# Gathering the ordered token ids with 48 and 16 rows in place of 43 and 2

## The chip, the cores and the metric

The program runs on one core of one Trainium2 chip. The time is the device time of one execution in microseconds (us). One execution is recorded by the hardware profiler; it has a span, from the first to the last instruction, and a time of its own that includes what lies around the span.

## What is computed

An attention layer with landmarks feeds a layer of experts in which each token goes to the one expert with the largest logit:

```python
# attention: q, k, v are (8, 8, 576, 64); 32 landmarks are means over 18 rows
A = softmax(q @ k_lm.T / 8); Bm = softmax(q_lm @ k_lm.T / 8); C = softmax(q_lm @ k.T / 8)
Z = Bm.T / (norm1(Bm) * norminf(Bm) + 1e-6)
for _ in range(6):
    Z = 2 * Z - Z @ Bm @ Z
x = (A @ Z @ C @ v)                        # then as rows: (4608, 512)
# experts: w_gate (512, 8), w1 (8, 512, 1024), w2 (8, 1024, 512)
expert_idx = argmax(x @ w_gate, axis=1)
gate_w = softmax(x @ w_gate)[arange(4608), expert_idx]
for e in range(8):
    mask = expert_idx == e
    out[mask] = gate_w[mask, None] * (relu(x[mask] @ w1[e]) @ w2[e])
```

## The kernel before

**First stage, up to about 259 us.** The attention is computed in 18 periods, pipelined over the 8 batches. Each batch writes its rows of x to a scratch tensor in HBM (`xs`) by plain transfers that SP issues. The order of the instructions in this stage is made by a scheduler that places them by its own estimate of times. In the last part of it (the tail of the attention) the orders of PE and SP are written out by hand.

**The table of ordered ids.** As soon as the logits of a batch are there, `tokens` works out for each token its place in a table `order` in HBM: 8 experts by 4608 places, 16 floats a place (the token's id, its gate weight, and zeros). `scatter` (L594) writes 96 places at a time from POOL, 6 such transfers a batch. 128 places in a row are one *block* of 8 KB, so a block holds the ids and gates of one tile of 128 tokens, all of one expert. The table has 288 blocks.

**Reading it back.** `rows_in` (L638 to L643) gathers whole blocks into SBUF by an indirect transfer from POOL: the list `at` has a block number for each partition, and block `at[p]` lands in partition `p` of the tile `room`. It is called twice. The early call, after 4 of the 8 batches, fetches the blocks of 2 tiles (`EARLY`) into `ids_early`. The other call, after the last scatter, fetches one block for each of up to 43 tiles (`SLOTS` = 36 + 8 - 1) into memory that later holds the second buffer of `ht`; in the trace it is `ht<-order,s_at`, in the early one `ids_early<-order,early_at`.

`rows` then turns the ids into row numbers for the gathers of x: four operations on DVE (L652, tile `r`), four transposes on PE (L656), a copy to integers on DVE (L659, tile `read`); later two more transposes (L666, L667) and copies (L670, L672) give the rows to write to and the gates.

**Second stage.** `Experts` goes over the tiles (slots). A slot's 128 rows of x are gathered by four indirect transfers from POOL (L820, into `xg` or `xe`), transposed in blocks on DVE (L833, `buf`), split into a high and a low part by ACT (L835) and DVE (L838, `xt`), and multiplied on PE with `w1` (`up`, L852, `ps_tp` and `ps_fi`). The relu on ACT (L870) and DVE (L872) gives `h`, which is turned in the same way to `ht`, multiplied with `w2` (`down`, `ps_fr` and `ps_ch`), scaled by ACT (L882) and scattered to the output by POOL (L883). Slots 0 and 1 use what the early call found; all others need the second gather. The weights of an expert are fetched by SP (L782, `raw`) and split by ACT (L796) and DVE (L797).

Between the two stages the order of all five engines is written by hand. On PE: `up` of slots 0 and 1, then the transposes of the ids, then `down` of slot 0. On DVE the operations L652 of the second gather stand ahead of L838 of slot 0, without which `down` of slot 0 can't begin. On POOL the gather stands behind the last scatter, and ahead of all gathers of x for slots 2 and up.

Of the kernel before, what the change touches and what calls it, by code (L numbers as in the profile page):

```python
# [12 lines left out]
F32 = mybir.dt.float32  # L13
# [19 lines left out]
REC = 16  # L33
# [22 lines left out]
def done(g):  # L56
    for _ in g:
        pass
# [422 lines left out]
EARLY = 2  # L481
# [4 lines left out]
class Routing:  # L486
# [150 lines left out]

    def rows_in(self, at, n):  # L638

        room = self.room[n][:n]  # L640
        self.ids = room.rearrange("p (a o) -> p a o", o=REC)
        self.nc.gpsimd.indirect_dma_start(out=room, out_offset=None, in_=self.blocks,
                                          in_offset=bass.IndirectOffsetOnAxis(ap=at[:n], axis=0))  # L643

    def rows(self, n, pad):

# [304 lines left out]
def moe(tc, q, k, v, wg, w1, w2, out):  # L951
    nc = tc.nc
    with ExitStack() as ctx, ExitStack() as late:
# [5 lines left out]
        with ExitStack() as zero:  # L959
            routing = Routing(tc, ctx, zero, psum, order)  # L960
        experts = Experts(tc, ctx, psum, routing, xs, w1, w2, out)
        experts.weights(ctx, 0)
        with ExitStack() as front:
            attention = Attention(tc, ctx, front, psum, q, k, v, wg)
            attention.tokens, attention.groups = routing.tokens, routing.groups
            attention.xs = [xs[S * b:S * b + S].rearrange("(p j) c -> p j c", j=J) for b in range(B)]
            routing.ident = attention.ident
            routing.room = {EARLY: front.enter_context(tc.tile_pool(name="r_ids", bufs=1)).tile([EARLY, REC * 128], F32, name="ids_early")}
            for i in range(2 * B + 2):
                extra = []  # L970
                if routing.scatters:
                    extra.append((routing.scattered(), J, 0))
                if i == ROWS:
                    done(routing.rows(EARLY, None))
                    extra.append((experts.start(), 8, 0))
                if i == 17:
                    extra.append((experts.split(0, 512, nc.vector), 8, 0))
                attention.period(i, B, extra)
                if i in CLEAR:
                    with tc.issue_after(attention.loads["v"].ins):  # L980
                        for e in CLEAR[i]:
                            routing.clear(e)
                if i == FETCH:
                    experts.fetch(0, routing.first[0:1, 0:1])
# [5 lines left out]
        with tc.manual_schedule(engines=engines):  # L990
# [12 lines left out]
            room = experts.buf[2].rearrange("p a c -> p (a c)")  # L1003
# [74 lines left out]
```

## Time and profile before

| | |
|---|---|
| median of 3 runs | 701.17 us (700.9 to 701.24) |
| the profiled execution, its own time | 700.81 us |
| its span | 699.0 us |
| PE busy | 647.4 us (93% of the span) |
| DVE busy | 521.5 us (75%) |
| ACT busy | 398.9 us (57%) |
| POOL busy | 345.2 us (49%) |
| HBM traffic | 124 GB/s over the span |

PE is the TensorE matmul engine, PEld its weight loads, DVE VectorE, ACT ScalarE, POOL GpSimd, SP SyncE. The profiled execution is 0.36 us below the median, and its span is 1.81 us shorter than its time; both differences are taken to stay as they are.

### The profile page before, as it was taken

What the parts mean: (1) busy time and instruction counts of PE and PEld (TensorE: products, weight loads), DVE (VectorE), ACT (ScalarE), POOL (GpSimd) and SP (SyncE); (2) the same over time, 40 slices, a digit from 0 to 9 for tenths busy, and PEclk for the clock granted to TensorE, in tenths of its full rate; (3) what the DMA queues carried; (4) which work ended last, traced back from release to release, by engine and by line L of the source; (5) the groups of instructions that cost most, each with busy time, mean ns of one, the idle gap of its engine ahead of it and who ended that gap; (6) DMA issues with size and microseconds to landing.
All of it is one profiled execution on the core that took longest, in us unless ns stands there. A gap on an engine that the chain in (4) does not pass through costs nothing.

```text
span 699.0 us, 13809 instructions
## 1 busy us (share of the span) xinstructions
PE 647.4 (93%) x4511; PEld 510.9 (73%) x4511; DVE 521.5 (75%) x1359; ACT 398.9 (57%) x983; POOL 345.2 (49%) x372
## 2 busy tenths in 40 slices
PE   7899989998898881999999999999999999999996
PEld 4676777666675661777888888888888888888884
DVE  4788876988878671667789879857599789866653
ACT  4776766575645461245577566645467477544442
POOL 4554546575363460777655354443536445351231
PEclk9999997998979995899999999999999999999999
DMA  9997766776342530146233423511143343310110
GB/s 221 292 276 178 205 159 146 197 200 207 96 111 59 181 85 20 60 144 224 72 121 122 137 92 128 166 51 43 57 155 116 105 137 107 126 62 31 31 49 30
DMA packets 47002, 87.35 MB, mean 125 GB/s; under 512 B 8642, under 2 KB 27074, under 8 KB 46851
## 3 DMA queue, kind: packets, MB, share of 16 engines
q1 hardware_dynamic: 36336, 65.30, 32.7%
q0 software_dynamic: 10560, 20.87, 9.5%
q8 instruction: 38, 0.62, 0.4%
q14 instruction: 68, 0.56, 0.3%
HBM read 64.61 MB, written 22.05 MB: 124 GB/s over the span
## 4 chain that ended last, share of the span: by engine, by line
PE 46%; DMA 3%; issue 3%; POOL 1%; DVE 1%; ACT 0%; POOLq 0%; DVEq 0%
PE ps_fi L852 12%; PE ps_ch L852 12%; PE ps_tp L852 11%; PE ps_fr L852 11%; DMA xe<-xs,read 3%; DVE h L872 0%; POOL xg L820 0%; POOL out_dram L883 0%; POOL xe L820 0%; DVE buf L833 0%; DVE ht L838 0%; ACT ht L835 0%; POOLq L918 0%; POOLq L883 0%; DVEq L833 0%
## 5 line engine op out<-in xcount | busy, mean ns | idle before, releaser
L883 POOL DMA_INDIRECT out_dram<-buf,write x38 | 39.0, 1026 | 166.0 <-ACTq L809 140.4
L820 POOL DMA_INDIRECT xg<-xs,read x80 | 83.7, 1046 | 42.3 <-issue 22.4
L820 POOL DMA_INDIRECT xe<-xs,read x84 | 88.0, 1047 | 25.7 <-issue 23.8
L835 ACT CAST ht<-buf 128x512 fp32r<-128x512 f32 x76 | 47.1, 622 | 87.9 <-DVE buf L833 86.9
L852 PE MATMUL ps_fr<-whi,ht 128*128 128x512 f32 x304 | 96.6, 399 | 0.0
L852 PE MATMUL ps_ch<-whi,ht 128*128 128x512 f32 x304 | 94.4, 392 | 2.4 <-ACTq L809 2.4
L852 PE MATMUL ps_tp<-whi,xt 128*128 128x512 f32 x304 | 83.2, 395 | 1.5 <-ACTq L809 1.5
L872 DVE TENSOR_SCALAR h<-ps_tp 32x256 f32<-32x256 f32 x152 | 64.2, 422 | 27.1 <-PE ps_tp L852 24.6
L872 DVE TENSOR_SCALAR h<-ps_fi 32x256 f32<-32x256 f32 x144 | 60.8, 422 | 28.8 <-PE ps_fi L852 26.5
L852 PE MATMUL ps_fi<-whi,xt 128*128 128x512 f32 x288 | 78.1, 393 | 0.0
L870 ACT ACTIVATE h<-ps_tp 32x256 f32<-32x256 f32 x152 | 57.1, 376 | 36.2 <-PE ps_tp L852 32.5
L870 ACT ACTIVATE h<-ps_fi 32x256 f32<-32x256 f32 x144 | 54.1, 376 | 34.8 <-PE ps_fi L852 31.0
L852 PEld LDWEIGHTS ps_ch<-whi,ht 128*128 128x128 f32 x304 | 57.0, 188 | 15.3 <-ACTq L809 3.2
L852 PEld LDWEIGHTS ps_fr<-whi,ht 128*128 128x128 f32 x304 | 58.2, 192 | 13.1 <-DVE ht L838 0.5
L852 PEld LDWEIGHTS ps_tp<-whi,xt 128*128 128x128 f32 x304 | 56.9, 188 | 14.2 <-ACTq L809 1.9
L852 PEld LDWEIGHTS ps_fi<-whi,xt 128*128 128x128 f32 x288 | 54.1, 188 | 11.8
L852 PE MATMUL ps_fr<-wlo,ht 128*128 128x512 f32 x152 | 60.5, 398 | 0.0
L852 PE MATMUL ps_ch<-wlo,ht 128*128 128x512 f32 x152 | 59.5, 391 | 0.0
L594 POOL DMA_INDIRECT order<-i_tok,l_at x48 | 45.5, 948 | 26.1 <-issue 11.2
L797 DVE TENSOR_TENSOR wlo<-raw,whi 128x512 fp32r<-128x512 f32 (+1 forms) x64 | 49.9, 834 | 5.7 <-ACT whi L796 5.7
L838 DVE TENSOR_TENSOR ht<-buf,ht 128x512 fp32r<-128x512 f32 x76 | 51.1, 692 | 3.8 <-ACT ht L835 0.2
L833 DVE STREAM_TRANSPOSE buf<-h 128x512 f32<-128x512 f32 x76 | 49.7, 690 | 5.6 <-DMA out_dram<-buf,write 1.8
(274 smaller groups left out, 1326.3 us busy)
## 6 DMA issues: line engine op xcount, KB each, us to landing
raw<-in_moe_w_dram SPq DMA_DIRECT2D x48, 512.0 KB, 5.8
ld_k<-in_k_dram SPq DMA_DIRECT2D x14, 576.0 KB, 5.3
ld_q<-in_q_dram SPq DMA_DIRECT2D x14, 576.0 KB, 7.7
ld_v<-in_v_dram SPq DMA_DIRECT2D x14, 576.0 KB, 5.0
xs<-xrow SPq DMA_DIRECT2D x40, 192.0 KB, 2.3
order<-zero SPq DMA_DIRECT2D x8, 288.0 KB, 10.7
xe<-xs,read POOLq DMA_INDIRECT x84, 2.6
xg<-xs,read POOLq DMA_INDIRECT x80, 2.8
```

Source lines behind the costliest of these rows:

```text
L594: self.nc.gpsimd.indirect_dma_start(out=self.places[n + j], out_offset=bass.IndirectOffsetOnAxis(ap=at[:, j:j + 1], axis=0), in_=self.tok[ ...
L797: (engine or nc.vector).tensor_tensor(out=l, in0=x, in1=h.bitcast(F32), op=ALU.subtract)
L820: self.nc.gpsimd.indirect_dma_start(out=x[:, t, :], out_offset=None, in_=src.rearrange("n (q c) -> (n q) c", q=4), in_offset=bass.Indirect ...
L833: nc.vector.transpose(out=x.rearrange("p c (t j) -> p t c j", t=4), in_=src[:, :, 32 * c:32 * c + 128].rearrange("p t (c i) -> p t c i", c=4))
L835: nc.scalar.copy(out=hi[:, c:c + 4, :], in_=x)
L838: nc.vector.tensor_tensor(out=lo[:, c:c + 4, :], in0=x, in1=hi[:, c:c + 4, :].bitcast(F32), op=ALU.subtract)
L852: nc.tensor.matmul(ps[c // 512] if type(ps) is list else ps[:, c // 512], lhsT=x0[:, a, :], rhs=w[:, a, c:c + 512], start=a == 0 and j == ...
L870: nc.scalar.activation(out=dst, in_=src, func=AF.Relu)
L872: nc.vector.tensor_scalar(out=dst, in0=src, scalar1=0.0, scalar2=None, op0=ALU.max)
L883: nc.gpsimd.indirect_dma_start(out=self.outs[s], out_offset=bass.IndirectOffsetOnAxis(ap=at, axis=0), in_=y, in_offset=None, bounds_check= ...
```

## The change

The length of the gathered list is rounded up to a multiple of 16: the second gather fetches 48 blocks into 48 partitions in place of 43, the early one 16 in place of 2, and the early tile has 16 partitions in place of 2. The added blocks are read and never used; everything that reads the tiles still takes 43 and 2 rows (`room[:n]`). The list `at` has 128 entries in both cases. An added entry is a valid block number: behind the last tile it is the number of its partition.

```diff
     def rows_in(self, at, n):
 
-        room = self.room[n][:n]
-        self.ids = room.rearrange("p (a o) -> p a o", o=REC)
+        m = -(-n // 16) * 16
+        room = self.room[n][:m]
+        self.ids = room[:n].rearrange("p (a o) -> p a o", o=REC)
         self.nc.gpsimd.indirect_dma_start(out=room, out_offset=None, in_=self.blocks,
-                                          in_offset=bass.IndirectOffsetOnAxis(ap=at[:n], axis=0))
+                                          in_offset=bass.IndirectOffsetOnAxis(ap=at[:m], axis=0))
...
-            routing.room = {EARLY: front.enter_context(tc.tile_pool(name="r_ids", bufs=1)).tile([EARLY, REC * 128], F32, name="ids_early")}
+            routing.room = {EARLY: front.enter_context(tc.tile_pool(name="r_ids", bufs=1)).tile([16, REC * 128], F32, name="ids_early")}
```

On POOL and SP no instruction changes its place. Here is POOL between the two stages, before (`order` is the table, `l_at` the places, `ht` the tile gathered into, `xg` and `xe` the rows of x):

```order
L594 DMA order<-i_tok,l_at 36864x16 x18
L642 DMA ht_4098<-order,s_at 43x2048
L820 DMA xg_4088<-xs,read_4417 128x128 x4
L820 DMA xg_4089<-xs,read_4417 128x128 x4
L883 DMA out_dram<-buf_4091,write_4461 4608x512
```

And with the change; the file is one line longer, so that L642 is L643 and L820 is L821:

```order
L594 DMA order<-i_tok,l_at 36864x16 x18
L643 DMA ht_4098<-order,s_at 48x2048
L821 DMA xg_4088<-xs,read_4417 128x128 x4
L821 DMA xg_4089<-xs,read_4417 128x128 x4
L884 DMA out_dram<-buf_4091,write_4461 4608x512
```

Only the size of the gather differs. In the first stage, from the early gather on, the scheduler orders PE, DVE and ACT a little differently. The first such place that matters for the last gather is DVE at the tail of the attention, where the places `l_at` of batch 5 are made, for which POOL's last run of scatters waits. Before (`l_t`, `l_mx` lead to `l_at`, `buf` holds rows of x or logits, `xt` the split rows of slots 0 and 1, `st` a tile of the values stage):

```order
L580 TENSOR_TENSOR l_t<-ps_fi,i_base 96x48
L339 TENSOR_TENSOR rp<-rp,ps_tp 128x2x32
L415 STREAM_TRANSPOSE buf_4093<-ps_fi 96x192
L838 TENSOR_TENSOR xt_4094<-buf_4091,xt_4094 128x512
L587 TENSOR_TENSOR acc<-acc,l_n 96x8
L279 COPY st<-ps_fr 128x8
L581 TENSOR_TENSOR l_t<-l_t,l_oh 96x48
L554 TENSOR_REDUCE l_mx<-buf_4093 96x6
L838 TENSOR_TENSOR xt_4095<-buf_4092,xt_4095 128x512
L582 TENSOR_REDUCE l_mx<-l_t 96x6
L555 TENSOR_TENSOR buf_4093<-buf_4093,l_mx 96x6x8
L583 CAST l_at<-l_mx 96x6
```

With the change:

```order
L580 TENSOR_TENSOR l_t<-ps_fi,i_base 96x48
L834 STREAM_TRANSPOSE buf_4091<-xe_144 128x4x4x32
L581 TENSOR_TENSOR l_t<-l_t,l_oh 96x48
L834 STREAM_TRANSPOSE buf_4092<-xe_145 128x4x4x32
L339 TENSOR_TENSOR rp<-rp,ps_tp 128x2x32
L582 TENSOR_REDUCE l_mx<-l_t 96x6
L415 STREAM_TRANSPOSE buf_4093<-ps_fi 96x192
L839 TENSOR_TENSOR xt_4094<-buf_4091,xt_4094 128x512
L583 CAST l_at<-l_mx 96x6
L554 TENSOR_REDUCE l_mx<-buf_4093 96x6
L839 TENSOR_TENSOR xt_4095<-buf_4092,xt_4095 128x512
```

L554, the second split of x (L838, now L839), L555 and an L279 stood ahead of `l_at` and now stand behind it; the two L833 (now L834) stood ahead of it in both. A little later on DVE the places `l_at` of batch 6 and the tile `w` of batch 7 are made, before (`wlo` is the split of `w2`):

```order
L580 TENSOR_TENSOR l_t<-ps_fi,i_base 96x48
L797 TENSOR_TENSOR wlo_4084<-raw_4082,whi_4083 128x512
L581 TENSOR_TENSOR l_t<-l_t,l_oh 96x48
L582 TENSOR_REDUCE l_mx<-l_t 96x6
L797 TENSOR_TENSOR wlo_4084<-raw_4082,whi_4083 128x512
L583 CAST l_at<-l_mx 96x6
L797 TENSOR_TENSOR wlo_4084<-raw_4082,whi_4083 128x512
L364 TENSOR_TENSOR w<-ps_ch,m_187 128x256 x2
```

With the change:

```order
L580 TENSOR_TENSOR l_t<-ps_fi,i_base 96x48
L581 TENSOR_TENSOR l_t<-l_t,l_oh 96x48
L582 TENSOR_REDUCE l_mx<-l_t 96x6
L798 TENSOR_TENSOR wlo_4084<-raw_4082,whi_4083 128x512
L583 CAST l_at<-l_mx 96x6
L364 TENSOR_TENSOR w<-ps_ch,m_187 128x256 x2
L798 TENSOR_TENSOR wlo_4084<-raw_4082,whi_4083 128x512 x2
```

One split of weights stands ahead of `l_at` in place of two, and one ahead of `w` in place of three. In the second stage the order of DVE differs in one pair (the second L838 of an early slot stands behind the first L872, not ahead of it).

## Rows read from the trace of the kernel before

**Rows 1.** The chain that ended last: start us, duration us, engine tile line.

```profile
317.54 5.73 PE ps_ch L852 x24
...
631.42 5.52 PE ps_fi L852 x24
```

**Rows 2.** Who waited for whom over the execution: us in total, times, longest us.

```profile
PE ps_fi L656 <- DVE r L652: 17.4, 1, 17.4
DVE r L652 <- DMA ht<-order,s_at: 15.5, 1, 15.5
POOL xg L820 <- DVE read L659: 18.4, 1, 18.4
```

**Rows 3.** Timeline, 259 to 279 us: start us, us, instruction, [idle before it <- releaser].

```profile
259.15 1.45 POOL L642 DMA_INDIRECT ht<-order,s_at  x1 [2.30 <-DVE h L872]
259.25 1.30 DVE L833 STREAM_TRANSPOSE buf<-h 128x512 f32<-128x512 f32 x2
261.23 3.17 ACT L870 ACTIVATE h<-ps_sc 32x256 f32<-32x256 f32 x8
276.08 1.18 DVE L652 SCALAR_TENSOR_TENSOR r<-ht,i_quarter 43x128 f32<-43x128 f32 x4 [15.53 <-DMA ht<-order,s_at]
...
279.01 0.97 POOL L820 DMA_INDIRECT xg<-xs,read  x1 [18.40 <-DVE read L659]
```

**Rows 4.** Windows between the stages: length, busy by engine, PEclk, DMA share, GB/s.

```profile
262.00:263.20 1.20, 0.00 (x0) 0.00 (x0) 0.00 (x0) 1.13 (x3) 0.00 (x0) 0.99 0.02 7
263.20:275.50 12.30, 0.00 (x0) 0.00 (x0) 0.00 (x0) 1.13 (x3) 0.00 (x0) 0.50 0.06 27
276.50:283.60 7.10, 7.02 (x19) 5.09 (x20) 6.07 (x17) 0.00 (x0) 3.68 (x4) 0.50 0.10 30
```

**Rows 5.** DMA queues and issues, 260 to 277 us: packets, MB, share of 16 engines.

```profile
q0 software_dynamic: 704, 0.35, 7.1%
ht<-order,s_at POOLq DMA_INDIRECT x1, 16.9
```

**Rows 6.** The same, 171.4 to 180.4 us, the early gather.

```profile
q0 software_dynamic: 32, 0.02, 1.3%
```

**Rows 7.** The same, 278.9 to 283.9 us, four gathers of x.

```profile
q0 software_dynamic: 96, 0.20, 13.0%
xg<-xs,read POOLq DMA_INDIRECT x4, 2.5
```

**Rows 8.** Timeline of DVE where the early ids are used.

```profile
180.41 0.34 DVE L652 SCALAR_TENSOR_TENSOR r<-ids_early,i_quarter 2x128 f32<-2x128 f32 x1
180.68 0.14 DVE L393 TENSOR_TENSOR l<-l,ps_fi 96x8 f32<-96x8 f32 x1
```

**Rows 9.** Timeline of POOL, 233 to 308 us.

```profile
233.92 0.94 POOL L594 DMA_INDIRECT order<-i_tok,l_at  x1 [8.95 <-DVE l_t L560]
241.42 1.11 POOL L594 DMA_INDIRECT order<-i_tok,l_at  x1 [0.45 <-DVE l_at L583]
255.94 0.92 POOL L594 DMA_INDIRECT order<-i_tok,l_at  x1 [0.30 <-issue]
...
306.36 0.94 POOL L820 DMA_INDIRECT xe<-xs,read  x1 [0.30 <-issue]
```

**Rows 10.** Timeline of DVE and PE, 308 to 318 us.

```profile
308.91 0.71 DVE L833 STREAM_TRANSPOSE buf<-xe 128x512 f32<-128x512 f32 x1 [4.30 <-DMA xe<-xs,read]
...
310.43 1.19 PE L852 MATMUL ps_tp<-whi,xt 128*128 128x512 f32 x4 [1.48 <-ACTq L809]
```

**Rows 11.** Timeline of DVE in the tail of the attention.

```profile
232.64 0.68 DVE L838 TENSOR_TENSOR xt<-buf,xt 128x512 fp32r<-128x512 f32 x1
233.47 0.17 DVE L583 CAST l_at<-l_mx 96x6 int32<-96x6 f32 x1
239.13 0.69 DVE L797 TENSOR_TENSOR wlo<-raw,whi 128x512 fp32r<-128x512 f32 x1 [3.04 <-ACT whi L796]
240.99 0.16 DVE L583 CAST l_at<-l_mx 96x6 int32<-96x6 f32 x1
```

## The prediction

> **What bounds the kernel now.** I read the chain that ended last first, to see which stretch is closed. From 317.54 us on it is PE alone, one product of 24 matmuls behind the other up to 637 us [rows 1]; nothing there can be gained by a faster transfer, but all of it starts earlier if the stretch ahead of it does. So I looked for the longest waits of PE in the list of waits. One stands out: 17.4 us for `r` on DVE, and DVE in its turn waits 15.5 us for the second gather of ids, POOL 18.4 us for what is made of it [rows 2]. It is one wait, seen by three engines.
>
> The timeline shows it from the inside [rows 3]. POOL issues the gather at 259.15, DVE is done with what it can do without it at 260.55 (259.25 + 1.30), ACT at 264.4 (261.23 + 3.17), and `r` starts at 276.08, 16.93 us after the issue. From there everything follows in a fixed order: POOL's first gather of x comes 2.93 us later, at 279.01.
>
> Why is the gather so slow? Between 263.2 and 275.5 the DMA engines are busy to a share of 0.06, which is 1 of 16, and move 27 GB/s [rows 4]. The queue's packets tell the same: 704 [rows 5]. 43 blocks on one engine, a small filler packet for each of them on the 15 others (645), and one completion packet on each of 16 make exactly 704. The early gather of 2 blocks has 32 packets [rows 6]: 2 blocks on 2 engines, 14 fillers, 16 completions; on one engine it would be 2 + 30 + 16 = 48. A gather of 128 rows of x has 32 (96 in a stretch with three of them) [rows 7], 16 of data and 16 completions. So 43 rows, a prime number, ran on 1 engine, 2 on 2 and 128 on 16.
>
> The Trainium skill, "DMA: Bandwidth & Descriptors", section "Why a DMA increments its semaphore by 16 and not by 1", says that the number of engines is the largest number up to 16 that divides the slowest dimensions of both sides; the trace agrees, with 1 engine for 43 rows. It also names an exception for some direct copies, which would have put 43 rows on 15 engines; the 704 packets speak against that here.
>
> **The change part by part.** *The second gather.* 48 rows spread over 16 engines are 3 blocks on each in place of 43 on one. A block takes 8,192 bytes / 27 GB/s = 0.303 us on one engine [rows 4]. No row shows this transfer, so I bound it from both sides.
> - Slow end: the same transfer without 40 of its 43 blocks on the busiest engine, 16.93 - 40 x 0.303 = 4.8 us from issue to landing.
> - Fast end: a gather of x lands 2.5 us after its issue [rows 7], with 4 KB an engine (0.15 us at 27 GB/s); with 24 KB (0.91 us) it is 2.5 + 0.76 = 3.3 us.
>
> The first is nearer, being the same transfer, but its issue took 1.45 us on POOL [rows 3], against 0.97 for a gather of x, which I put down to its 704 packets; 64 packets should save about half a microsecond of it. I take 4.2 us. DVE then starts `r` at 259.15 + 4.2 = 263.35, behind its own 260.55, so the wait shrinks to 2.8 us and doesn't vanish. Gain: 16.93 - 4.2 = **12.7 us**, between 12.1 and 13.6. The five added blocks are in this; on DVE and PE nothing gets larger.
>
> The skill's same page, section "Anatomy of one DMA", fits 2.0 us plus bytes / 436e3. For 393,216 bytes that would be 2.9 us, an estimate from that page, and the sum would be 1.3 us better than mine; for the 352,256 bytes of before it gives 2.8 us against the 16.93 measured, so it holds at best for a transfer that is spread.
>
> *What is behind it.* DVE's and PE's steps from `r` on are the same, and ACT is free at 264.4, before DVE's next `h` is due. POOL's gathers of x start 2.93 us after `r` as before, and then POOL issues transfer upon transfer, 22 from 279.01 to 306.36 (1.3 us each), the last of them the rows of slot 5 [rows 3, 9]. DVE waits 4.30 us for these rows at 308.91, and PE, whose next operand stands behind that on DVE, idles 1.48 us at 310.43 [rows 10]. So POOL, not PE, carries the shift through, and it carries all of it. What is late next is POOL's row of gathers.
>
> *The clock of PE.* After the last matmul PE's granted clock stayed at 1.00 (2.4 GHz) to 263.2 us and was at 0.50 (1.2 GHz) from there through 283.6, 7 us after PE resumed [rows 4]. PE would now resume at about 263.9, near the moment at which it fell. If the clock stays up, PE does its 7.1 us of half-clock work up to 3.5 us faster, but then it waits that much longer at the place of rows 10. I cost it at nothing; the cover is POOL's row of issues.
>
> *The early gather.* 16 blocks of 8 KB on 16 engines in place of 2 on 2. Its landing is not waited for: DVE takes `r` at 180.41 behind other work, 9 us after the issue [rows 8]. The 14 added blocks (115 KB) run at a time when the queues are full; at 16 engines x 27 GB/s they hold the others up by at most 0.3 us. Taken at nothing; the cover is those 9 us.
>
> *The scheduler's other order.* That is the part of the change that isn't meant. In the tail the last gather can't be issued before the last scatter (255.94) has landed, and the 18 scatters run back to back on POOL from 233.92, when the first `l_at` (233.47) is there [rows 9, 11]. In the new order four DVE operations that stood ahead of this first `l_at` stand behind it (an L838 of 0.68 us [rows 11], and an L279, an L554 and an L555 of 0.15 to 0.20), so it comes up to 1.2 us earlier. The next group's `l_at` (240.99) stood behind two splits of weights, the first of which waited 3.04 us for ACT [rows 11]; now it stands behind one, and so is ready about 1.1 us earlier too. Against that, PE's last matmuls on `v`, after which SP may fetch `w2` into that memory, stand a few instructions later in PE's new order. I take **0.7 us** gained. But from the early gather on (171 us) DVE, PE and ACT run in another order for 60 us, with clock and waits following from it, and no row prices that: I allow 3 us either way.
>
> *Sum.* 700.81 - 12.7 - 0.7 = 687.4 us for the profiled execution (span 685.6). The median of before is 0.36 above its profile, so the forecast is **687.8 us**.
>
> **The rivals.**
> 1. *The gather still runs on one engine* (slower than before). If the number of engines came from something else than the count of rows, such as the size of a block, 48 blocks would take 5 x 0.303 = 1.5 us more: 701.17 + 1.5 - 0.7 = 702.0, or 702.7 if the other order gives nothing. It decides at one question, whether 48 rows are divided by 16; the counts for 2, 43 and 128 rows speak against it. Chance 0.04.
> 2. *The first stage gives part of it back.* If the new order costs more than 3 us ahead of the last scatter, because a `l_at` or the fetch of `w2` comes late, the time is 688.5 + 3 to 688.5 + 7: 691.5 to 695. For it speaks that PE, DVE and ACT wait for one another there at every step; against it that the two places I could follow both move forward. Chance 0.10.
> 3. *PE carries the end after all and its clock stays up.* Then up to 3.5 us of the half-clock stretch come on top: 687.8 - 3.5 = 684.3. Against it stands the idle time of PE in rows 10, which shows that POOL is later. Chance 0.05.
>
> **How the numbers follow.** The forecast has a chance of 0.81; by its own terms (12.1 to 13.6 gained on the gather, the order 0.7 gained give or take 3) it goes from 684 to 692, most of it within 686 to 690. The likeliest single time is 687.8. The range that holds 8 in 10 reaches into rival 2 and rival 3: **684.7 to 691.8**. A difference under 0.2% (1.4 us) can't be told from no change in this kernel. Faster by more than that: the forecast, rivals 2 and 3, 0.95; within 0.2%: 0.02, half of rival 1's prices; slower: 0.03.
>
> **What would show it.** Right: the second gather has 64 packets, the DMA share over its time is several tenths, and it lands 3.3 to 4.8 us after its issue; DVE's wait for it falls from 15.5 to about 2.8 us and PE's for `r` from 17.4 to about 4.7; the first gather of x comes 2.9 us after `r`; PE still idles over 1 us ahead of `up` of slot 4. The issue of the second gather moves by the first stage's part, forecast 0.7 us earlier. Wrong: a DMA share of 0.06 again (rival 1), an issue of the gather at 262 us or later (rival 2), or PE without that idle time and its clock at 1.00 throughout (rival 3).

## The result, and the profile after

The changed kernel takes 690.75 us (median of four runs, 688.39 to 692.17) against 701.03 of the kernel before beside it (four runs, 698.57 to 701.24); the ratio is 0.9853, with a 95% interval of 0.9823 to 0.9883. The forecast was 687.8 us, with a range of 684.7 to 691.8. The profiled execution took 688.39 us and has a span of 686.6 us, 12.4 us less than before. All lines from L640 on carry a number that is one higher.

The list of waits, with the three rows that answer to [rows 2]:

```profile
POOL xg L821 <- DVE read L660: 7.4, 1, 7.4
PE ps_fi L657 <- DVE r L653: 5.7, 1, 5.7
DVE r L653 <- DMA ht<-order,s_at: 3.8, 1, 3.8
```

All three are 11 to 12 us shorter, and none is gone. The timeline that answers to [rows 3]:

```profile
258.90 0.90 POOL L643 DMA_INDIRECT ht<-order,s_at  x1 [2.17 <-issue]
259.13 1.30 DVE L834 STREAM_TRANSPOSE buf<-h 128x512 f32<-128x512 f32 x2
261.11 3.18 ACT L871 ACTIVATE h<-ps_sc 32x256 f32<-32x256 f32 x8
264.26 1.19 DVE L653 SCALAR_TENSOR_TENSOR r<-ht,i_quarter 43x128 f32<-43x128 f32 x4 [3.83 <-DMA ht<-order,s_at]
...
267.18 0.96 POOL L821 DMA_INDIRECT xg<-xs,read  x1 [7.38 <-DVE read L660]
```

The gather now is on POOL for 0.90 us in place of 1.45, and `r` starts at 264.26, **5.36 us after the issue** in place of 16.93. This time, from POOL's issue of the gather to the start of `r`, is called the landing below. POOL's first gather of x follows 2.92 us after `r`, as before (2.93). The DMA view of the 5.5 us from the issue to just behind `r` (the two upper rows are 40 slices of 0.14 us: busy share of the 16 engines in tenths, and GB/s), which answers to [rows 4, 5] (a packet counts in the slice in which it begins):

```profile
DMA  0000000002099985559947940030000000000000
GB/s 0 0 0 0 0 0 0 0 0 60 0 298 417 179 238 179 119 119 536 238 60 119 238 60 0 0 60 0 0 0 0 0 0 0 0 0 0 0 0 0
...
q0 software_dynamic: 64, 0.39, 34.9%
```

There are 64 packets, 48 of data and 16 completions, as forecast. 34.9% of 16 engines over 5.5 us are 30.7 us of packets: **0.64 us for a block** at most, where one engine alone took 0.303. POOL's scatters ahead of the gather and the last gather of x behind it, which answer to [rows 9]:

```profile
233.93 1.25 POOL L594 DMA_INDIRECT order<-i_tok,l_at  x1 [10.88 <-DVE l_mx L554]
...
255.81 0.92 POOL L594 DMA_INDIRECT order<-i_tok,l_at  x1 [0.30 <-issue]
...
294.39 0.94 POOL L821 DMA_INDIRECT xe<-xs,read  x1 [0.30 <-issue]
```

The waits of DVE and PE ahead of the chain, and the chain, which answer to [rows 1, 10]:

```profile
296.94 0.71 DVE L834 STREAM_TRANSPOSE buf<-xe 128x512 f32<-128x512 f32 x1 [4.26 <-DMA xe<-xs,read]
...
298.46 1.21 PE L853 MATMUL ps_tp<-whi,xt 128*128 128x512 f32 x4 [1.50 <-ACTq L810]
...
305.42 0.72 PE L853 MATMUL ps_ch<-whi,ht 128*128 128x512 f32 x2 [1.18 <-ACTq L810]
```

```profile
305.42 5.75 PE ps_ch L853 x24
...
619.17 5.53 PE ps_fi L853 x24
```

Everything here is shifted as a whole: POOL's last gather for slot 5 by 11.97 us (306.36 to 294.39), DVE's wait for the rows of slot 5 by 11.97 us (308.91 to 296.94), PE's wait behind it by 11.97 (310.43 to 298.46), the start of the chain that is PE alone by 12.12 (317.54 to 305.42), the end by 12.4. PE's wait ahead of slot 4 is the same, 1.50 us against 1.48.

In one place PE's clock is lower than before. The windows of the changed kernel (busy time of PE, PEld, DVE, ACT and POOL with their counts; then PE's granted clock, the share of the DMA engines, GB/s):

```profile
226.30:233.10 6.80, 6.80 (x81) 4.89 (x79) 4.64 (x16) 2.72 (x7) 0.00 (x0) 0.55 0.13 23
261.00:264.50 3.50, 0.00 (x0) 0.00 (x0) 0.24 (x1) 3.09 (x9) 0.00 (x0) 0.53 0.35 68
264.50:271.00 6.50, 6.24 (x16) 4.57 (x16) 6.13 (x16) 0.00 (x0) 2.91 (x4) 0.50 0.07 23
271.00:284.00 13.00, 13.00 (x59) 10.49 (x59) 8.27 (x24) 3.79 (x6) 10.13 (x10) 0.98 0.21 66
```

From 226.3 to 233.1, in the tail of the attention, the clock was at 0.55 on average, so mostly at 1.2 GHz. The same window of the kernel before has it at 1.00:

```profile
226.30:233.10 6.80, 6.68 (x103) 5.46 (x103) 6.80 (x28) 3.72 (x11) 0.00 (x0) 1.00 0.33 97
```

What stands ahead of it on PE is a wait that the kernel before hasn't got:

```profile
225.42 0.78 PE L321 MATMUL ps_tp<-rp 128*128 128x160 f32 x4 [1.15 <-DVE l_m L562]
```

After the gather the clock fell as before, but only to about 271, not to 283.6.

### The profile page after: what moved, and what is told of

Read it like the earlier page. It is cut to its first block, busy times and chain, and to the rows that moved or that the text cites. A ratio compares the mean times of both kernels' runs of the same rounds, so it can differ in the third digit from the quotient of the medians.

```text
span 686.6 us, 13812 instructions
## 1 busy us (share of the span) xinstructions
PE 647.9 (94%) x4511; PEld 509.9 (74%) x4511; DVE 520.8 (76%) x1359; ACT 398.9 (58%) x983; POOL 343.9 (50%) x372
## 3 DMA queue, kind: packets, MB, share of 16 engines
q1 hardware_dynamic: 36336, 65.30, 33.1%
## 4 chain that ended last, share of the span: by engine, by line
PE 46%; DMA 4%; issue 3%; DVE 1%; POOL 1%; ACT 0%; POOLq 0%; DVEq 0%
PE ps_fi L853 12%; PE ps_ch L853 12%; PE ps_tp L853 11%; PE ps_fr L853 11%; DMA xg<-xs,read 4%; DVE h L873 0%; POOL out_dram L884 0%; POOL xg L821 0%; DVE buf L834 0%; DVE ht L839 0%; ACT ht L836 0%; POOLq L919 0%; POOLq L884 0%; DVEq L834 0%; DVEq L810 0%
## 5 line engine op out<-in xcount | busy, mean ns | idle before, releaser
L821 POOL DMA_INDIRECT xe<-xs,read x84 | 87.5, 1042 | 25.7 <-issue 24.1
L821 POOL DMA_INDIRECT xg<-xs,read x80 | 83.7, 1046 | 31.3 <-issue 21.8
L594 POOL DMA_INDIRECT order<-i_tok,l_at x48 | 45.7, 952 | 27.7 <-issue 11.5
L839 DVE TENSOR_TENSOR ht<-buf,ht 128x512 fp32r<-128x512 f32 x76 | 51.0, 691 | 3.8 <-ACT ht L836 0.2
L834 DVE STREAM_TRANSPOSE buf<-h 128x512 f32<-128x512 f32 x76 | 49.7, 692 | 4.9 <-DMA out_dram<-buf,write 1.0
```

The source lines that it names most:

```text
L594: self.nc.gpsimd.indirect_dma_start(out=self.places[n + j], out_offset=bass.IndirectOffsetOnAxis(ap=at[:, j:j + 1], axis=0), in_=self.tok[ ...
L821: self.nc.gpsimd.indirect_dma_start(out=x[:, t, :], out_offset=None, in_=src.rearrange("n (q c) -> (n q) c", q=4), in_offset=bass.Indirect ...
L834: nc.vector.transpose(out=x.rearrange("p c (t j) -> p t c j", t=4), in_=src[:, :, 32 * c:32 * c + 128].rearrange("p t (c i) -> p t c i", c=4))
L839: nc.vector.tensor_tensor(out=lo[:, c:c + 4, :], in0=x, in1=hi[:, c:c + 4, :].bitcast(F32), op=ALU.subtract)
```

## The experiments

Two theories. **Mine:** the number of engines that carry the second gather is the largest number up to 16 that divides its rows; going from 1 to 16 is the whole gain, and what is behind it only shifts. **Rivals:** part of the gain (rival A), or a loss that hides some of it (rival B), is in the early gather and in the other order of the first stage; or the size of the list counts and not its divisors (rival C); or PE's clock, not POOL's transfers, carries the end (rival 3 of the prediction).

Where a group of kernels ran side by side, the kernel before ran among them. Its mean was 698.64 us (17 runs) for the first group and 699.49 (11 runs) for the third. The second group fell on a chip on which the kernel before took 752 us and the gather was issued at 290 to 294 us; I use only landings and ratios from it.

**1. The two parts apart.** One kernel with 48 rows in the second gather and 2 in the early one, whose order in the first stage is that of the kernel before; one with 16 in the early gather and 43 in the second, whose order is that of the changed kernel; and the changed kernel again.

The edit for the second gather of 48 alone (the early tile has its 2 partitions again):

```diff
-        m = -(-n // 16) * 16
+        m = 2 if n == EARLY else 48
```

> Only the second gather takes 48 rows, the early one stays at 2, and the order of the first stage is that of the kernel before. My theory (the spread of the second gather over 16 engines is the whole gain, the other order of the first stage only moves the time by some us): 64 packets, landing 5.3 to 5.5 us after the issue as in the changed kernel, so 701.0 - 11.6 = 689.4 us, and runs as close together as those of before. Rival A (the early gather or the other order carries part of the gain): the time stays above 692. Rival B (the other order costs something, which the second gather has to pay for): over 1 us faster than the changed kernel in the same call.

> The second gather of 48 alone again, as the base of the three others of this call. Landing 5.1 to 5.4 us after the issue, ratio to before 0.983. Mean time within 1.5 us of the changed kernel if the other order costs nothing, 2 us below it if it costs here what it cost with 43 rows (1.0032).

Its timeline, POOL and DVE, in the first of the two:

```profile
258.33 0.90 POOL L643 DMA_INDIRECT ht<-order,s_at  x1 [2.16 <-issue]
...
263.47 1.19 DVE L653 SCALAR_TENSOR_TENSOR r<-ht,i_quarter 43x128 f32<-43x128 f32 x4 [3.60 <-DMA ht<-order,s_at]
```

And in the second, with PE's waits behind:

```profile
257.98 0.90 POOL L643 DMA_INDIRECT ht<-order,s_at  x1 [2.16 <-DVE buf L834]
...
262.89 1.19 DVE L653 SCALAR_TENSOR_TENSOR r<-ht,i_quarter 43x128 f32<-43x128 f32 x4 [4.60 <-DMA ht<-order,s_at]
...
297.32 1.20 PE L853 MATMUL ps_tp<-whi,xt 128*128 128x512 f32 x4 [2.15 <-ACTq L810]
304.44 0.72 PE L853 MATMUL ps_ch<-whi,ht 128*128 128x512 f32 x2 [1.34 <-ACTq L810]
```

It lands 5.14 and 4.91 us after the issue, a little sooner than expected. Ratios to before: 0.9835 (0.9787 to 0.9883) and 0.9842 (0.9799 to 0.9886), or 11.5 and 11.1 us. So this one edit is the whole gain; rival A falls. The runs are not closer together than those of the changed kernel (681.96 to 689.16, and 684.48 to 691.58): that expectation was wrong.

The early gather of 16 alone:

```diff
-        m = -(-n // 16) * 16
+        m = 16 if n == EARLY else 43
```

> Only the early gather takes 16 rows, the second one stays at 43; the order of the first stage is that of the changed kernel. My prediction's step (the order gains 0.7 us): 700.3 us. Neutral order: 701.0, within 1.4. Rival B (the order costs what the changed kernel lacks to 701.0 - 11.6 = 689.4 against its 690.75): about 702.4. Rival A (part of the gain is here): below 698. In all of them the second gather has 704 packets and lands 16.9 us after its issue.

```profile
261.28 1.46 POOL L643 DMA_INDIRECT ht<-order,s_at  x1 [2.30 <-DVE h L873]
...
278.18 1.18 DVE L653 SCALAR_TENSOR_TENSOR r<-ht,i_quarter 43x128 f32<-43x128 f32 x4 [15.51 <-DMA ht<-order,s_at]
```

The landing is 16.90 us, as before. The time is not better: ratio 1.0032 (1.0001 to 1.0062), 2.2 us longer. PE in its tail, with the clock in the window behind the wait:

```profile
227.37 0.78 PE L321 MATMUL ps_tp<-rp 128*128 128x160 f32 x4 [1.16 <-DVE l_m L562]
...
228.40:235.20 6.80, 6.80 (x80) 4.90 (x80) 4.69 (x15) 2.61 (x7) 0.00 (x0) 0.56 0.17 30
```

This is the picture of the changed kernel: the same wait for `l_m`, and the half clock behind it.

The changed kernel, twice more:

> The changed kernel once more, beside the two that do one part of it each. If its runs differ by 3.8 us again (688.4 to 692.2) the spread belongs to it; the profiled landing of the second gather is 5.4 us again if the 4.2 of the prediction was mis-sized, and 4 to 5 us if the profile of it caught a late packet.

> The changed kernel, for the price of the other order beside the run of 48 alone. If the order costs a half-clock stretch of PE in the tail: PE's clock at 0.50 for some 6 us between 225 and 240 us, after a wait for `l_m` of DVE, as in the three profiles of this order so far, and none there in the run of 48 alone; mean time 2 us above that one. If what PE loses there comes back later: the same stretch, and the same mean time.

Ratios 0.9826 (0.9781 to 0.9871) and 0.9854 (0.9817 to 0.9891), landings 5.42 and 5.51 us, so the first profile had not caught a late packet. In means, it is 0.2 and 0.9 us longer than 48 alone beside it (687.42 against 687.24, 689.08 against 688.19; six runs each). In the first repeat the clock was at 0.55 behind the wait, as in the other two profiles of this order; in the second it was not:

```profile
226.66 0.78 PE L321 MATMUL ps_tp<-rp 128*128 128x160 f32 x4 [1.15 <-DVE l_m L562]
...
227.60:234.40 6.80, 6.12 (x98) 4.59 (x96) 6.20 (x23) 4.04 (x11) 0.90 (x1) 1.00 0.33 107
```

The wait of 1.15 us is in all four profiles of the new order and in none of the old one; the half clock follows in three of four. But such a stretch is not peculiar to the new order: without that wait, three profiles of the old one have a stretch of it a few us earlier (from 215 to 220 and from 220 to 225, 48 alone is at 1.00 and 0.66, 47 rows at 0.67 and 0.65, the kernel of experiment 4 on the third group's chip at 0.50 and 0.84), where the kernel before and 48 alone in its second run are at 1.00. **The price of the new order stays open between 0 and 2 us:** 2.2 us beside the gather of 43, whose interval only just leaves out no difference, and 0.2 and 0.9 beside that of 48, where means of six runs can't tell 0 from 2.

**2. What sets the number of engines.** Lists of 47 rows (a prime), 46 and 128, the early gather at 2; the further blocks are read and not used. The edit for 47:

```diff
-        m = 2 if n == EARLY else 48
+        m = 2 if n == EARLY else 47
```

> Only the second gather is changed, to 47 rows, a prime number. My theory (the engines are the largest number up to 16 that divides the rows): one engine, 47 + 47 x 15 + 16 = 768 packets, landing 16.93 + 4 x 0.303 = 18.1 us after the issue, 702.2 us in all. Rival C (five more blocks, or some other effect of a larger list, spread the transfer, whatever divides it): some 64 packets, landing near 5.4 us, 689.5 us.

The DMA queue and the timeline of 47 rows:

```profile
q0 software_dynamic: 768, 0.39, 6.5%
```

```profile
262.58 1.51 POOL L643 DMA_INDIRECT ht<-order,s_at  x1 [2.30 <-DVE buf L834]
...
280.88 1.18 DVE L653 SCALAR_TENSOR_TENSOR r<-ht,i_quarter 43x128 f32<-43x128 f32 x4 [18.13 <-DMA ht<-order,s_at]
```

768 packets, as counted beforehand, and 18.30 us to `r`. Four blocks more than 43 and one less than 48, and nothing is gained: the size of the list isn't it. Its one run took 705.56 us, 3.4 more than the 702.2 expected; the gather was issued 3.43 us later than in the kernel before (262.58 against 259.15), so the difference stands ahead of it.

> Second gather of 46 rows, early one at 2. If the engines are the largest number up to 16 that divides the rows: 2 engines with 23 blocks each, 46 + 14 x 23 + 16 = 384 packets, landing 16.93 - 20 x 0.303 = 10.9 us after the issue, an issue on POOL between 0.90 and 1.46 us, about 695 us in all. If only prime lists run on one engine and all others are spread as well as can be: some 64 packets and a landing near 5.3 us.

The same views of 46 rows:

```profile
q0 software_dynamic: 384, 0.38, 9.6%
```

```profile
292.97 1.19 POOL L643 DMA_INDIRECT ht<-order,s_at  x1 [2.29 <-ACT h L871]
...
304.28 1.18 DVE L653 SCALAR_TENSOR_TENSOR r<-ht,i_quarter 43x128 f32<-43x128 f32 x4 [8.31 <-DMA ht<-order,s_at]
```

384 packets and 11.31 us: 2 engines, with 23 blocks each. It is not that primes alone are slow. What 46, 47 and 48 rows do not separate from my rule is a rival one, the largest power of two up to 16 that divides the rows: it gives the same 2, 1 and 16 engines, and the same for 2, 43 and 128. No kernel here ran a list that would tell them apart (45 rows: 15 engines or 1).

> Second gather of 128 rows, early one at 2; the 80 further blocks are read and not used. 8 blocks an engine in place of 3. If a block costs 0.303 us as on one engine: landing 5.1 to 5.4 + 5 x 0.303 = 6.7 us after the issue. If 16 engines together are slower by block (3 blocks took 2.2 us, 0.73 us each): 5.3 + 5 x 0.73 = 8.9 us, and the 4.2 of my prediction failed on that; if the landing moves by less than 0.8 us, it is a fixed part that was too small.

The same of 128 rows (the upper row has slices of 0.2 us):

```profile
DMA  0000000000009593979399699694401000000000
...
q0 software_dynamic: 144, 1.05, 39.2%
```

```profile
293.74 0.97 POOL L643 DMA_INDIRECT ht<-order,s_at  x1 [2.16 <-ACT h L871]
...
299.76 0.92 DVE L653 SCALAR_TENSOR_TENSOR r<-ht,i_quarter 43x128 f32<-43x128 f32 x3 [2.00 <-DMA ht<-order,s_at]
```

6.02 us for 2.7 times the blocks of 48: below both expectations, and 0.75 above the 5.27 that is the mean of all seven landings of 48. The packets took 50.2 us (39.2% of 16 engines over 8 us), 0.39 us for a block. So 0.64 is not a fixed price of a block when 16 engines work. The trace shows where the dear ones are: the 25 blocks that begin before 296.4 took 17.0 us, 0.68 each, and the 103 behind them 33.1 us with the completions, 0.32 each, hardly more than the 0.303 of one engine alone. The chip isn't the reason: 48 rows on the same chip (the kernel of experiment 4 in this group) took 30.2 us of packets, 0.63 for a block, and landed after 5.28 us.

**3. Smaller blocks.** A place in the table gets 8 floats in place of 16 (the id, the gate and zeros), so that a block is 4 KB; 48 rows, early 2. The scatters write half as much, and the scheduler gives the first stage an order of its own.

```diff
-REC = 16
+REC = 8
...
-        room = self.room[n][:m]
+        room = self.room[n][:m, :REC * 128]
```

> As the second gather of 48 alone, but a place of the table has 8 floats in place of 16, so that a block is 4 KB; the scatters write 32 bytes in place of 64, and the scheduler's order changes too. If bytes set the landing (0.303 us a block on one engine, or 0.73 with 16): 0.45 to 1.1 us earlier than 5.1 to 5.4, so 4.0 to 4.9 us; if a fixed part does: within 0.3 us of 5.2. The time follows by at most that, 687 to 690 where before is 699, unless the order or the smaller scatters cost something.

> The table with blocks of 4 KB, once more beside its base. If the 0.64 us that a block of 8 KB took with 16 engines at work is what my 4.2 us lacked: landing 4.0 to 4.4 us after the issue, near my number, and DVE's wait 1 us shorter than in the base; time 1 us below the base, if the other order and the smaller scatters cost nothing. If a fixed part is what it lacked: landing 5.0 or more.

On the chip of the second group DVE was not free until 298.22, 4.26 us after the issue, and did not wait any more; ratio 0.9828 (0.9801 to 0.9855). In the third group:

```profile
q0 software_dynamic: 64, 0.20, 8.9%
```

```profile
257.80 0.90 POOL L643 DMA_INDIRECT ht<-order,s_at  x1 [2.14 <-issue]
...
261.56 1.25 DVE L653 SCALAR_TENSOR_TENSOR r<-ht,i_quarter 43x128 f32<-43x128 f32 x4 [2.21 <-DMA ht<-order,s_at]
```

3.76 us, 1.15 earlier than its base (4.91) and 1.5 below the mean of 48 blocks of 8 KB. 8.9% of 16 engines over 8 us are 11.4 us, 0.24 us for a block. That is below the 4.0 to 4.4 expected if the price of a block was at fault, and far below the 5.0 of a fixed part: the landing follows the bytes. The time is 687.18 us in the mean against 688.19 of the base, ratio to before 0.9829 (0.9792 to 0.9867): about the 1 us expected, but not to be told from the base by these runs.

**4. PE kept busy.** 20 products of the identity on PE in the wait for the ids, to take away the fall of its clock; 48 rows, early 2.

```diff
+        for _ in range(20 * (n == SLOTS)):
+            nc.tensor.matmul(ps[:, :128], lhsT=self.ident, rhs=self.ident, start=True, stop=True)
         for t in range(4):
             nc.tensor.transpose(ps[:, n * t:n * t + n], r4[:, t]...
```

> As the second gather of 48 alone, with 20 products of the identity (128 x 128) on PE ahead of the transposes of the ids, so that PE works through most of its wait. My step (POOL's row of transfers carries the end, the clock is worth nothing): PE's clock stays at 1.00 past 264, PE is ahead by up to 2.5 us, and its wait ahead of `up` of slot 4 grows by as much, from 2.35 us to some 4 to 5; time as that of 48 alone, ratio 0.983. Rival 3 (the half clock is paid for): 2.5 to 3.5 us faster, ratio 0.979, with the wait ahead of slot 4 unchanged.

> The 20 products on PE during the wait, once more beside its base. My step (POOL's row of transfers carries the end): clock 1.00 until after the ids are there, PE's wait ahead of slot 4 grows from some 2 us by what PE gains, time as the base within 1 us. Rival 3 (the half clock is paid for): 2.5 to 3.5 us below the base.

On the chip of the second group the ratio is 0.9821 (0.9794 to 0.9848), beside 0.9828 of the half blocks. In the third group, the windows (PE's clock before the last two columns):

```profile
258.00:264.00 6.00, 6.00 (x47) 5.63 (x46) 3.24 (x7) 3.04 (x7) 0.90 (x1) 1.00 0.35 71
264.00:270.00 6.00, 4.91 (x23) 3.31 (x22) 4.73 (x13) 1.17 (x4) 1.61 (x2) 1.00 0.03 10
270.00:285.00 15.00, 14.42 (x64) 11.21 (x63) 9.57 (x28) 3.79 (x6) 11.34 (x13) 1.00 0.21 62
...
303.00:312.00 9.00, 4.57 (x11) 3.37 (x12) 4.17 (x9) 4.14 (x10) 6.77 (x8) 0.72 1.02 363
```

The clock is at 1.00 from 258 to 285, where the base has 0.60 from 264 to 270. PE and DVE (the products stand under L657, x40):

```profile
259.92 4.63 PE L657 MATMUL ps_fi<-ident 128*128 128x128 f32 x40
265.57 1.09 PE L659 MATMUL ps_fi<-ident,r 43*128 43x43 f32 x4 [1.02 <-DVE r L653]
...
303.67 0.73 PE L855 MATMUL ps_ch<-whi,ht 128*128 128x512 f32 x2 [1.27 <-ACTq L812]
...
307.34 0.71 DVE L836 STREAM_TRANSPOSE buf<-xg 128x512 f32<-128x512 f32 x1 [3.74 <-DMA xg<-xs,read]
308.16 0.79 PE L855 MATMUL ps_ch<-wlo,ht 128*128 128x512 f32 x1 [3.76 <-DVEq L812]
```

PE reaches `ps_ch` with `ht` 38.52 us after `r` (265.15 to 303.67), 3.03 us sooner than the base (262.89 to 304.44, 41.55). Then it waits 3.76 us, behind DVE, which waits 3.74 us for a gather of x, while the DMA engines are full (a share of 1.02, 363 GB/s). POOL issued its last gather into `xg` ahead of this wait 35.7 us after `r` (300.84), and in the base 35.5 us after it (298.41): POOL's row does not follow PE. Behind the wait the clock is at 0.50 from 306.9 to 313.7, and PE needs 7.86 us for 22 products, where the base has 5.75 for 24:

```profile
308.16 7.86 PE ps_ch L855 x22
```

The time is 690.06 us in the mean against 688.19, ratio to before 0.9858 (0.9815 to 0.9901): nothing gained. It is 1.9 us longer where within 1 us was expected, which six runs can't tell from no difference. Rival 3 falls. The wait came two steps later than I expected, at the rows of the next slot and not ahead of slot 4.

**The parts of the span.** The profiles side by side, in us: issue of the second gather, from there to `r`, from `r` to the first product of the chain that is PE alone, and from there to the end.

| kernel | issued | landing | to the chain | to the end | span |
|---|---|---|---|---|---|
| before | 259.15 | 16.93 | 41.46 | 381.5 | 699.0 |
| changed | 258.90 | 5.36 | 41.16 | 381.2 | 686.6 |
| changed, again | 261.77 | 5.42 | 41.21 | 381.6 | 690.0 |
| changed, third | 258.92 | 5.51 | 41.16 | 381.3 | 686.9 |
| 48 alone | 258.33 | 5.14 | 41.48 | 381.0 | 685.9 |
| 48 alone, again | 257.98 | 4.91 | 41.55 | 381.3 | 685.7 |
| early 16 alone | 261.28 | 16.90 | 41.24 | 381.5 | 700.9 |
| 47 | 262.58 | 18.30 | 41.48 | 381.4 | 703.8 |
| 48 of 4 KB | 257.80 | 3.76 | 41.46 | 381.2 | 684.2 |
| 48, PE busy | 259.86 | 5.29 | 43.01 | 383.3 | 691.5 |

The last two parts are constant within 0.7 us but for the kernel that keeps PE busy, which has the longer wait and the half clock behind it. What differs beside the landing is the first stage, by up to 4.8 us from profile to profile, in the same kernel too (258.90 and 261.77).

## Why the prediction was right, step by step

- **What bounds the kernel:** right. A wait seen by three engines; it fell by 11.7 us for DVE and PE and 11.0 for POOL, and the time followed. That the engines follow what the number of rows can be divided by, and not its size, is shown by 47, 46 and 48 rows: 768, 384 and 64 packets, which is 1, 2 and 16 engines. The Trainium skill's rule ("DMA: Bandwidth & Descriptors", section "Why a DMA increments its semaphore by 16 and not by 1") counts the largest number up to 16 that divides the slowest dimensions, and the runs agree with it three times. They would agree as well with the largest power of two that divides the rows.
- **The second gather:** the mechanism was right, the size off. The term was 4.2 us, bounds 3.3 to 4.8; it measured 5.36, and 5.27 in the mean of seven profiles, outside the bounds. Each part can be checked now. The issue was to save half a microsecond, and saved 0.55. The three blocks were set at 0.303 us each from a row in which one engine worked; in this short transfer they took up to 0.64. 3 x (0.64 - 0.303) = 1.0 us, and 4.2 + 1.0 = 5.2. Halving the bytes gives 1.15 to 1.5 us back. But that this sum fits is in part luck. By the working of the prediction the last block ends 16.47 - 12.73 = 3.74 us after the issue (16.47 in the kernel before) and `r` follows 0.46 us behind it (275.62 to 276.08). In the changed kernel the last block begins at 262.52, takes 0.79 and ends 4.40 us after the issue, and `r` follows 0.96 us behind it; in the seven profiles of 48 rows of 8 KB that is 0.76 to 1.25. So 0.66 us of what the term lacked lie ahead of the end of the last block, and 0.50 behind it, which I had taken over unchanged. The slow bound was no bound for the same two reasons. Gain: 11.6 us in place of 12.7.
- **The sum by the Trainium skill:** the Trainium skill's "DMA: Bandwidth & Descriptors", section "Anatomy of one DMA", gave 2.9 us for these bytes, an estimate, and is 2.4 us short of the 5.27 measured.
- **What is behind it:** right. From `r` to the chain it takes 41.46 us before and 41.16 after, whether PE's clock is back at 284 or at 271.
- **PE's clock at nothing:** right, for the reason given. With the clock kept at 1.00 through that stretch, PE gains 3.03 us and waits 3.76 us for gathered rows, which POOL issues at the same distance from `r`. PE's resuming "near the moment at which it fell" was wrong: the clock fell at about 261 in place of 263.2, and then stayed low to about 271.
- **The early gather at nothing:** nothing contradicts it. POOL is on it for 0.92 to 0.94 us with 2 or 16 rows, and the kernel that has only this edit differs in the first stage alone; its own price can't be told from that of the order which comes with it.
- **The scheduler's other order, 0.7 us gained:** not borne out. The three comparisons (2.2, 0.2 and 0.9 us longer) all go the other way, though only the first is clear of noise, and only just. Of the two `l_at` that I followed, the first was to be up to 1.2 us earlier and the second about 1.1. They came at 233.49 in place of 233.47 and at 241.03 in place of 240.99, although the early gather was issued 2.25 us earlier in this profile (169.18 against 171.43), ahead of every moved instruction. From the early gather to the first of the 18 scatters that follow it takes 63.2 to 64.8 us in the four profiles of the new order, and 60.3 to 65.0 in five of the old one (means 64.3 and 63.0). What I had not seen is the wait of PE for `l_m`, and the half clock that stands behind it in three of four profiles. I read the order for what moved forward, at two places, and not for what PE waits for.
- **The sum:** 13.4 us forecast, 12.4 in the profiles, of which 11.6 is the landing, 0.25 the issue, and some 0.6 lies behind. The profile of the changed kernel was the fastest of its four runs (688.39, median 690.75), so the 0.36 us by which I went from profile to median did not hold: executions of one kernel lie 4 to 10 us apart here.
- **Rivals:** one engine is out (64 packets). Rival 2 came close in the median (690.75, and it began at 691.5), but over 3 us lost to the order is not what the runs show. Rival 3 is out by the wait of 1.50 us and by the kernel that keeps PE busy.

## What to carry to other kernels

Give an indirect gather a number of rows that 16 divides, even if the further rows are thrown away: here five useless blocks of 8 KB bought 11.6 us, and with one row less (47) all of it was gone. Count the packets of a queue to see on how many engines a transfer ran, and don't take the time of a block in a long transfer on one engine for that of three blocks on each of sixteen. Where a scheduler orders the program, an edit can move instructions far from it; make only the edit that pays (here the second gather), and compare by many runs, since one profile against another says little below the spread of the stage ahead.

## What the runs showed of the hardware beyond what was expected

- POOL's time for issuing this gather grows with its packets: 0.90 us for 64, 0.97 for 144, 1.19 for 384, 1.46 for 704 and 1.51 for 768, so by some 0.9 ns a packet (an estimate, 0.61 / 704). A gather of 32 packets is no cheaper than one of 64: the early one took 0.92 to 0.94 us.
- A block of 8 KB took 0.303 us on one engine, up to 0.64 when 16 engines fetched 3 each, and up to 0.39 when they fetched 8 each; one of 4 KB up to 0.24. In the transfer of 8 it is the first blocks that are dear (0.68 against 0.32), on a chip where 3 an engine cost 0.63. What makes them dear is not settled.
- From the end of the last block to the start of the DVE operation that waits for it, 0.46 us passed with 43 rows, 0.76 to 1.25 with 48, 0.42 with 128, and 0.68 with 48 of 4 KB. Nothing here shows what sets it.
- PE's granted clock fell to 0.50 behind a wait of 1.15 us in three of four profiles and stayed at 1.00 in the fourth, with PE's instructions in the same order; three of five profiles without that wait have a stretch of 0.50 a few us earlier. Nothing here shows what decided it.
